# Spectral mixing, maxima scans and softmax attention in one loop of equal two-step rounds over five single PSUM banks

## The chip, the cores and the metric

The kernel runs on one core of one Trainium2 chip. The metric is the device time of one execution in microseconds (us). Five engines work at once, each through its own queue in order: TensorE (PE, matrix products; its weight loads are shown apart as PEld), VectorE (DVE), ScalarE (ACT), GpSimd (POOL) and SyncE (SP, which here only starts transfers). Matrix products are written to PSUM, which holds eight banks of 128 x 512 floats.

## The reference

One input x of 2048 rows and 512 columns goes through two mixers, and a gate per row blends them. `A_wqkv` and `A_wo` are multiplied by 64 in the set-up, so the scores are large and the softmax needs its row maxima.

```python
g = _sigmoid((x * gate_w).sum(-1, keepdims=True))
# A: softmax attention, 32 heads of width 16
q, k, v = (x @ wqkv) split in three, per head
scores = jnp.einsum("bhqd,bhkd->bhqk", q, k) * scale
p = _softmax(scores, axis=-1)
a = (p @ v over the heads) @ wo
# B: Fourier mixing, real part of a two-dimensional transform
ar = jnp.einsum("bsd,ed->bse", x, dft_hid_re)
ai = jnp.einsum("bsd,ed->bse", x, dft_hid_im)
b = jnp.einsum("ts,bse->bte", dft_seq_re, ar) - jnp.einsum("ts,bse->bte", dft_seq_im, ai)
return g * a + (1 - g) * b
```

## The kernel before

All products but one kind take operands split in two parts, hi and lo, and add three products (hi*hi, hi*lo, lo*hi). They contract over at most 64 rows, so PE is used as two row groups: j=0 in rows 0 to 63 and j=1 in rows 64 to 127. The two matmuls of a pair, one for each group, are issued side by side and run together, each with its own PSUM bank. The text counts such pairs. The exception is the product of probabilities and values (`pv`): it contracts over 128 rows, its output has 17 columns (16 values and the sum), and four of them, one for each `(c, j)`, run side by side in column groups and add up in one bank, `pvb`.

The work of a head pair p (16 of them) on PE: 64 "scans", each a pair of 128 x 512 score blocks whose row maxima are needed before the exponentials can be taken; then 32 "steps" (two query halves h, sixteen key blocks kb). A step has two score pairs (c=0 and 1), four 128 x 512 blocks of exponentials on ACT, and one `pv` group. The scans of a head pair must be done, and its maxima stored and loaded again as extra rows of the operands, before its steps begin. The spectral part has 2 phases (real and imaginary) of 16 output blocks t, each 48 pairs long (16 blocks s, three products); its coefficients are loaded in units of 4 blocks s and split into hi and lo ahead of use. At the end, the attention output is multiplied by `wo` (`mix_heads`, `mix_rest`) and added to the spectral rows.

The order of the work is written out by hand; the queues follow it. It has three parts.

1. Projections (960 pairs: q, k, v and the two hidden transforms). From the ninth block on, scans are put between the products by `beside`, one after every `PACE` = 3.9 product pairs. These scans are plain: one bank pair (`s1`), one DVE maximum over 128 x 1024 (L136).
2. 24 of the 32 spectral blocks, 1152 pairs, with 500 more scans between them, one after every 2.19 product pairs. These are "folded": ACT copies the positive part of one 128 x 512 block to SBUF (L157), and one DVE instruction folds the next block into it and takes the maximum (L159); every block has a single bank of its own (`d0`, `d1`, `k0`, `k1`). After parts 1 and 2 a total of `FRONT` = 692 of the 1024 scans are done.
3. A loop of 512 steps. Each step issues the score pair c=0 into a double bank (one ACT instruction over 1024, L220), while scans are left one scan pair, the score pair c=1 into two single banks of three (two ACT instructions of 512, L687), and the `pv` group of the step before (L693). From step `MIX` = 333, when no scans are left, the eight other spectral blocks and then the output products fill the place, three pairs a step, and `pv` is issued for two steps at once every other step.

After each query half, `quotients` (L702, L705) copies `pvb` to SBUF and sends its sums out through POOL's queue, and some steps later `divide` (L711 to L728) inverts them, brings them back through two transfers, multiplies and stores the rows. Most of `divide` is in POOL's queue. In part 3 the coefficient units are split on DVE (L809, L810).

Of the kernel before, what the change touches and what calls it, by code (L numbers as in the profile page):

```python
# [18 lines left out]
P = 128  # L19
S = 2048  # L20
# [14 lines left out]
LATER = 8  # L35
FRONT = 564 + 16 * LATER
PACE = 3.9
FOLDED = range(3 * SCANS, FRONT)
FOLD_PACE = 2.19
NARROW = 5.3  # L40
NWARM = 20
MIX = TOTAL - FRONT + 1
OUT = MIX + NB * LATER
SLOW = 3
SCANS_IN = 0
AHEAD = (9, 11, 14)


def build(tc, x, xT, wqkv, wo, wrT, wiT, cr, ci, gate, out):
    nc = tc.nc  # L50
    with ExitStack() as ctx:
        keep = ctx.enter_context(tc.tile_pool(name="keep", bufs=1))
        stk = ctx.enter_context(tc.tile_pool(name="stk", bufs=6))
# [4 lines left out]
        psf = ctx.enter_context(tc.tile_pool(name="psf", bufs=1, space=PSUM, reuse_waits="tile"))  # L58
# [3 lines left out]
        ks_d = [dram.tile([P, S], F32, name=f"ks_d{f}") for f in range(ND)]  # L62
        kf_d = [dram.tile([P, 2, S], F32, name=f"kf_d{f}") for f in range(ND)]
        m_d = [dram.tile([2, 4, 2, NB, 32], F32, name=f"m_d{p}") for p in range(NP)]
        ab_d = [[dram.tile([P, D], F32, name=f"ab_d{i}_{t}") for t in range(NB)] for i in range(2)]
        y_d = [dram.tile([P, 4, D], F32, name=f"y_d{c}") for c in range(NC)]
# [19 lines left out]
        scanned, used, unfolded = {}, {}, {}  # L86

        def row_loads(p, queue, keys=k_d):

            qs = stk.tile([P, S], F32R, tag="stk", name="qs")  # L90
            ks = stk.tile([P, S], F32R, tag="stk", name="ks")
# [9 lines left out]
        def load_scan(p):  # L101
            if p < NP:
                scanned[p], loads = row_loads(p, nc.sync)
                for load in loads:
                    load()

        def load_use(p):
            if p < NP:
                used[p], loads = row_loads(p, nc.sync)
                for load in loads:  # L110
                    load()
                qs, ks = used[p]
                for j in range(2):
                    b = 64 * j + 48
                    nc.sync.dma_start(ks[b:b + 2, :].bitcast(F32), ones_d)
                    for n in range(2):
                        nc.sync.dma_start(qs[b + n:b + n + 1, :].bitcast(F32),
                                          m_d[p][n:n + 1, :, j].rearrange("n g b k -> n b g k"))
# [6 lines left out]
        def scan(n, ps):  # L125

            p, i = n // SCANS, n % SCANS
            qb, c = i // 4, i % 4
            qs, ks = scanned[p]
            if i == 0:  # L130
                new_maxima(p)
            for j in range(2):
                b = 64 * j
                nc.tensor.matmul(ps[:, j, :], qs[b:b + 48, qb * P:(qb + 1) * P],  # L134
                                 ks[b:b + 48, c * 512:(c + 1) * 512], start=True, stop=True)
            nc.vector.tensor_reduce(mx[p][:, :, qb, c], ps, axis=AX.X, op=ALU.max)  # L136

        fold = [None, None]

        def scan_folded(n, j, bank, pool):  # L140

# [3 lines left out]
            if i == 0 and j == 0:  # L147
                new_maxima(p)
                if p == FRONT // SCANS:
                    nc.gpsimd.memset(mx[p], -3.0e38)  # L150
# [4 lines left out]
            if c % 2 == 0:  # L155
                fold[j] = pool.tile([P, 512], F32, tag=f"fold{j}", name="fold")
                nc.scalar.activation(fold[j], ps, AF.Relu)  # L157
            else:
                nc.vector.tensor_tensor_reduce(out=fold[j], in0=ps, in1=fold[j], scale=1.0, scalar=-3.0e38,  # L159
                                               op0=ALU.add, op1=ALU.max, accum_out=mx[p][:, j, qb, c // 2:c // 2 + 1])  # L160

        def shift(p):
# [10 lines left out]
            of = mx[p].rearrange("p j b c -> p (j b) c")[:, :, 0:2 if p * SCANS in FOLDED and (p + 1) * SCANS <= FRONT else 4]  # L173
# [15 lines left out]
        turns = [0]  # L189

        def wide(i, name):
            return psf.tile([P, 2, 512], F32, tag=f"wide{i}", name=name)

# [7 lines left out]
        both = []  # L201

        def qk(p, h, kb, c, pss):

            q0 = h * 1024 + c * 512
            qs, ks = used[p]
            for j in range(2):
                b = 64 * j
                nc.tensor.matmul(pss[j], ks[b:b + 50, kb * P:(kb + 1) * P],  # L209
                                 qs[b:b + 50, q0:q0 + 512], start=True, stop=True)  # L210

        def qk_both(p, h, kb, c=0):

            ps = wide(1 - SCANS_IN, "s3")
            qk(p, h, kb, c, [ps[:, j, :] for j in range(2)])
            if len(both) < 4:
                both.append(ring4.tile([P, 2, 512], F32, tag="c", name="eb"))
            e = both[ebs[0] % 4]
            ebs[0] += 1
            nc.scalar.activation(e, ps, AF.Exp, scale=SCALE)  # L220
            return [e[:, j, :] for j in range(2)]

        ebs, ahead, sums = [0], [], []

# [3 lines left out]
        with ExitStack() as pf:  # L228

            def s1():  # L230
                return pss1[0].tile([P, 2, 512], F32, tag="s1", name="s1")

            pss1 = []

            def xy():
                turns[0] += 1
                ps = wide(turns[0] % 2, "xy")
                return ps[:, 0, :], ps[:, 1, :]
# [15 lines left out]
            def load_scan_beside(p):  # L254
                scanned[p], loads = row_loads(p, nc.scalar if p else nc.sync, kf_d if p * SCANS in FOLDED else k_d)
                for n, load in enumerate(loads):
                    after(7 * n, load)
# [4 lines left out]
            def beside():  # L262
# [6 lines left out]
                if seen[0] == FOLDED[0] and not beds:  # L269
                    pace[1] = 0.0  # L270
                while seen[0] < FRONT and pace[1] >= 1.0:
                    pace[1] -= 1.0
                    n = seen[0]
                    if n % SCANS == 36 and n - n % SCANS + SCANS < FRONT:
                        load_scan_beside(n // SCANS + 1)
                    if n not in FOLDED:
                        done = scan_plain(n)
                    else:

                        scan_folded(n, 0, *beds)  # L280
# [8 lines left out]
            beds = []  # L289

            def behind(n):
                if n in FOLDED:
                    scan_folded(n, 1, *beds)
                    return n

            def scan_plain(n):
                if not beds:
                    scan(n, s1())
                    return n
                p, i = n // SCANS, n % SCANS  # L300
                qs, ks = scanned[p]
                for j in range(2):
                    ps, b = beds[0](f"{'dk'[n % 2]}{j}"), 64 * j
# [27 lines left out]
            coef = []  # L331
            for ph, plain, pair in ((0, range(NB - 2), (NB - 2, NB - 1)), (1, range(2, NB), (0, 1))):
                split_up = [(ph, t, u) for half in range(2) for t in pair for u in (2 * half, 2 * half + 1)]
                whole = [(ph, t, u) for t in plain for u in range(NU)]
                coef += split_up + whole if ph else whole + split_up
            coef = coef[:len(coef) - NU * LATER]
            craw, ready = {}, {}

            def load_coef(n, raw):
                ph, t, u = coef[n]  # L340
                craw[n] = raw
                nc.sync.dma_start(raw, (cr, ci)[ph][t, :, u * CS:(u + 1) * CS, :])

# [707 lines left out]
```

## Time and profile before

| | |
|---|---|
| runs | 1746.61, 1746.79, 1747.98 us; median 1746.79 |
| profiled execution, span | 1747.7 us |
| granted PE clock | 0.998 of full speed |
| part 1 | 0 to 289.6 us |
| part 2 | 289.6 to 688.5 us |
| part 3 with scans | 688.5 to 1328.0 us |
| part 3 with spectral blocks and outputs | 1328.0 to 1728.5 us |
| after the last round | 1728.5 to 1747.7 us |

The span of the profiled execution is 0.9 us above the median of the runs and inside their spread, so sums are made against 1747.7. PE is marked busy almost everywhere; a busy PE need not be at its peak, since a matmul's record also covers its waits inside the engine. What counts is how far the starts of pairs lie apart. An idle time in a row stands in square brackets with what ended it.

### The profile page before, as it was taken

The page shows a single profiled execution, that of the slowest core. Times are in us where ns is not written, and L with a number is a line of the kernel's source. Part 1 is how long each engine was busy: PE and PEld are TensorE (multiplying, and loading weights), DVE is VectorE, ACT ScalarE, POOL GpSimd, SP SyncE. Part 2 cuts the span into 40 slices and gives each one's busy share as a digit, 9 for nine tenths or more (in the row PEclk, how much of TensorE's full clock was granted, in tenths as well). Part 3 has the DMA queues.
Part 4 walks back from the last instruction along what each step waited for, and adds up shares of the span by engine and source line. Part 5 has one row for each costly group of instructions (what it writes and reads, how often), then busy time and mean ns, then how long its engine had stood idle before and what let it go on. Part 6 is the DMA issues. An engine that isn't in the chain of part 4 may idle for free.

```text
span 1747.7 us, 35504 instructions
## 1 busy us (share of the span) xinstructions
PE 1717.2 (98%) x13640; PEld 1020.7 (58%) x13640; DVE 1154.7 (66%) x1876; ACT 1451.8 (83%) x2383; POOL 712.4 (41%) x814
## 2 busy tenths in 40 slices
PE   8999999999999999999999999999999999999998
PEld 6887787888888887333333333333334555555554
DVE  6799999999999887666666666666664212222333
ACT  5445345888888787999999999999999888888885
POOL 3678667555556664032323323232232322322222
PEclk9999999999999999999999999999999999999999
DMA  8792666343345445432332513515313254255712
GB/s 293 258 299 77 191 196 210 114 118 116 102 151 151 140 133 112 82 65 57 60 65 56 90 34 71 87 24 96 78 35 74 65 116 90 69 141 139 175 36 100
DMA packets 126809, 199.54 MB, mean 114 GB/s; under 512 B 54016, under 2 KB 56560, under 8 KB 119728
## 3 DMA queue, kind: packets, MB, share of 16 engines
q1 hardware_dynamic: 84368, 161.02, 35.0%
q0 software_dynamic: 38496, 19.47, 5.1%
q10 hardware_dynamic: 3776, 16.78, 3.6%
q8 instruction: 107, 1.75, 0.4%
q14 instruction: 62, 0.51, 0.1%
HBM read 133.04 MB, written 63.71 MB: 113 GB/s over the span
## 4 chain that ended last, share of the span: by engine, by line
PE 86%; DMA 5%; DVE 3%; POOL 2%; issue 2%; ACT 1%; SPq 0%; DVEq 0%; POOLq 0%; ACTq 0%
PE pvb L693 27%; PE xy L184 21%; PE s L209 18%; PE s L184 8%; PE s L153 7%; PE s L134 6%; DMA lc<-ob 2%; DVE mx L136 2%; DMA fa<-ks_d 1%; DMA kf_d<-fa 1%; POOL s L252 1%; DMA raws<-xT 1%; DMA raws<-wqkv 0%; POOL el L252 0%; POOL fa L252 0%
## 5 line engine op out<-in xcount | busy, mean ns | idle before, releaser
L136 DVE TENSOR_REDUCE mx<-s 128x2 f32<-128x1024 f32 x524 | 627.1, 1222 | 204.6 <-PE s L134 204.6
L220 ACT ACTIVATE eb<-s 128x1024 f32<-128x1024 f32 x513 | 575.6, 1122 | 55.7 <-PE s L209 55.5
L687 ACT ACTIVATE e<-s 128x512 f32<-128x512 f32 x1022 | 604.4, 699 | 2.1 <-PE s L209 2.1
L693 PE MATMUL pvb<-eb,va 128*17 128x512 f32 x2052 | 515.9, 597 | 0.0
L693 PE MATMUL pvb<-e,va 128*17 128x512 f32 x2044 | 515.0, 597 | 0.0
L209 PE MATMUL s<-qs,ks 50*128 50x512 f32 x2048 | 427.2, 436 | 0.0
L209 PEld LDWEIGHTS s<-qs,ks 50*128 50x128 f32 x2048 | 210.2, 184 | 367.8 <-ACT eb L220 279.1
L184 PE MATMUL xy<-b,c 64*128 64x512 f32 x2640 | 418.4, 393 | 0.3 <-ACT c L318 0.3
L159 DVE CUSTOM_DVE_ANT_0 fold<-s,fold 128x512 f32<-128x512 f32 x500 | 338.5, 690 | 38.4 <-PE s L153 18.8
L157 ACT ACTIVATE fold<-s 128x512 f32<-128x512 f32 x500 | 295.7, 601 | 69.8 <-PE s L153 43.3
L184 PEld LDWEIGHTS xy<-b,c 64*128 64x128 f32 x2640 | 296.7, 187 | 19.9 <-ACT c L318 0.6
L153 PE MATMUL s<-ks,qs 48*128 48x512 f32 x1000 | 224.5, 405 | 6.7 <-DVE mx L159 5.1
L134 PE MATMUL s<-ks,qs 48*128 48x512 f32 x1048 | 223.1, 396 | 6.2 <-DVE mx L136 4.7
L705 POOL DMA_DIRECT2D lc<-ob x124 | 63.1, 515 | 304.7 <-DVE ob L702 304.3
L693 PEld LDWEIGHTS pvb<-eb,va 128*17 128x17 f32 x2052 | 69.1, 95 | 192.1 <-issue 183.4
L153 PEld LDWEIGHTS s<-ks,qs 48*128 48x128 f32 x1000 | 121.5, 184 | 46.4 <-DVE mx L159 17.4
L712 POOL DMA_DIRECT2D r_d<-lc x31 | 18.1, 585 | 293.3 <-DVE lc L711 284.5
L350 POOL TENSOR_TENSOR c<-craw,c 128x512 fp32r<-128x512 f32 x92 | 120.0, 1304 | 7.4
L134 PEld LDWEIGHTS s<-ks,qs 48*128 48x128 f32 x1048 | 108.0, 183 | 18.0 <-DVE mx L136 9.1
L349 POOL CAST c<-craw 128x512 fp32r<-128x512 f32 x92 | 56.3, 612 | 141.2 <-PE xy L184 137.3
L184 PE MATMUL xy<-w,b 64*128 64x512 f32 x768 | 105.2, 392 | 0.2 <-ACT s L414 0.2
L436 ACT ACTIVATE tx<-xy 128x512 f32<-128x512 f32 x48 | 28.7, 598 | 76.0 <-PE xy L184 50.2
(126 smaller groups left out, 1527.4 us busy)
## 6 DMA issues: line engine op xcount, KB each, us to landing
craw<-ci SPq DMA_DIRECT2D x64, 256.0 KB
craw<-cr SPq DMA_DIRECT2D x60, 256.0 KB
ks<-k_d SPq DMA_DIRECT2D x46, 256.0 KB
qs<-q_d SPq DMA_DIRECT2D x46, 256.0 KB
ab_d<-ab SPq DMA_DIRECT2D x32, 256.0 KB
y_d<-y SPq DMA_DIRECT2D x32, 256.0 KB
o_d<-oh POOLq DMA_DIRECT2D x28, 256.0 KB, 9.7
o_d<-ol POOLq DMA_DIRECT2D x28, 256.0 KB, 11.4
```

The source lines that it names most:

```text
L134: nc.tensor.matmul(ps[:, j, :], qs[b:b + 48, qb * P:(qb + 1) * P], ks[b:b + 48, c * 512:(c + 1) * 512], start=True, stop=True)
L136: nc.vector.tensor_reduce(mx[p][:, :, qb, c], ps, axis=AX.X, op=ALU.max)
L153: nc.tensor.matmul(ps, qs[b:b + 48, qb * P:(qb + 1) * P], ks[b:b + 48, c * 512:(c + 1) * 512], start=True, stop=True)
L157: nc.scalar.activation(fold[j], ps, AF.Relu)
L159: nc.vector.tensor_tensor_reduce(out=fold[j], in0=ps, in1=fold[j], scale=1.0, scalar=-3.0e38, op0=ALU.add, op1=ALU.max, accum_out=mx[p][:, ...
L184: nc.tensor.matmul(ps[j], lhs[r], rhs[r], start=first, stop=last)
L209: nc.tensor.matmul(pss[j], ks[b:b + 50, kb * P:(kb + 1) * P], qs[b:b + 50, q0:q0 + 512], start=True, stop=True)
L220: nc.scalar.activation(e, ps, AF.Exp, scale=SCALE)
L350: sub(lo, raw, hi.bitcast(F32))
L687: nc.scalar.activation(e[j], pss[j], AF.Exp, scale=SCALE)
L693: nc.tensor.matmul(pvb[r:r + VC, :], va[:, kb, 2 * p + j, :], es[c][j], start=kb == 0, stop=kb == NB - 1, tile_position=(0, r))
L705: nc.gpsimd.dma_start(lc[32 * n:32 * n + 32, :], ob[r + DH:r + VC, :].rearrange("p (s e) -> p s e", e=16))
```

## The change

All 32 spectral blocks move into the loop, and of the scans only 320 (`FRONT = 5 * SCANS`) stay ahead of it: 64 plain ones, now with two DVE maxima of 512, and 256 folded ones, all between the projections, the folded ones one after every 2.08 product pairs, the first scan 22 product pairs earlier than before. Part 2 is gone. The loop runs over 256 rounds of two steps. A round issues the eight score matmuls of its two steps (`e`), up to four scan pairs (`c`, plain, each matmul with a DVE maximum of 512 of its own), and 6, 7 or 9 pairs of spectral or output products (`s`), in an order given by `ORDERS` for the numbers of scan pairs and product pairs; the two matmuls of a pair are separate entries, so that one row group may be ahead of the other. Then it issues the `pv` groups of the two steps of the round before.

PSUM in the loop is eight single banks: `pvb`, `z0` and `z1` for the products of the two row groups, and `b0` to `b4` for scores and scans together. `Banks` keeps the planner's own clock and gives each score or scan the bank that it takes to be free first. Every exponential is one ACT instruction of 512 into one of 15 tiles.

The built order holds 157 rounds with three scan pairs, 57 with four, 3 with one or two and 39 with none (17 of these with six product pairs, 3 with seven, 19 with nine), in all 704 scan pairs, 1024 score pairs and 1725 product pairs.

The coefficient units are split on POOL (L214, L215). The hi and lo parts of the second phase's operands are made on POOL during the first phase (`part_b`, L872, L873), stored to `bs_d`, and loaded when the first phase's last block has used the old ones (`renew`). Row operands are loaded when two of six slots come free (`prefetch`). In the projections the sums of two key blocks are formed from tiles that are still on the chip instead of being loaded again (`fold_keys`). The scratch for POOL's transfers is set to 8192.

```diff
-FRONT = 564 + 16 * LATER
+FRONT = 5 * SCANS
 PACE = 3.9
-FOLDED = range(3 * SCANS, FRONT)
-FOLD_PACE = 2.19
+FOLDED = range(SCANS, FRONT)
+FOLD_PACE = 2.08
+MACROS = STEPS // 2
+ORDERS = {
+    (3, 7): "e1 c0 s1 e0 c1 s0 e1 s0 s1 s0 c1 s0 e0 s1 s0 c1 s0 e1 s1 c0 s1 s0 e0 s1 s1 e0 c0 e1",
+    (3, 6): "e1 c0 e1 s0 s0 e0 c1 s0 s1 s1 c0 e0 s1 s1 e0 c1 s0 s1 s0 e1 e0 e1 s0 s1 c0 c1",
+    (4, 6): "c1 e0 e0 e1 s1 c0 s0 s1 s1 e0 c1 s0 c1 s0 e1 s0 c0 e1 c0 s1 s1 s0 s0 e1 s1 c0 e0 c1",
+    (4, 7): "c0 e1 c1 s0 e0 e1 s1 s0 s0 s1 c1 e0 s1 s0 c1 s0 e0 e1 s0 c0 s1 e0 s1 s1 s0 c0 e1 s1 c1 c0",
...
+}
...
-                after(84, scan_at, PACE)
+                after(62, scan_at, PACE)
...
+            def scan_plain(n):
...
+                for j in range(2):
+                    ps, b = narrow(f"{'dk'[n % 2]}{j}"), 64 * j
+                    nc.tensor.matmul(ps, qs[b:b + 48, i // 4 * P:(i // 4 + 1) * P],
+                                     ks[b:b + 48, i % 4 * 512:(i % 4 + 1) * 512], start=True, stop=True)
+                    nc.vector.tensor_reduce(mx[p][:, j, i // 4, i % 4:i % 4 + 1], ps, axis=AX.X, op=ALU.max)
...
+            for tag in ("b0", "b1", "b2", "b3", "z0", "z1", "b4"):
+                bank(tag)
+            pvb = bank("pv", "pvb")
...
+            class Banks:
+
+                slot, late, gap, load, group = 230.0, 434.0, 106.0, 200.0, 854.0
+                period, release = {"e": 477.0, "c": 600.0}, {"e": 750.0, "c": 740.0}
...
+                    s = max(self.t, self.rows[j])
+                    if kind != "s":
+                        b = min(range(5), key=lambda b: self.free[b])
+                        s = max(s, self.free[b])
+                        a = max(self.engine[kind], s + self.late)
+                        self.engine[kind], self.free[b] = a + self.period[kind], a + self.release[kind]
+                    self.t, self.rows[j] = s + 4.0, s + self.slot
...
+            def score(j):
...
+                ps = bank(banks.take("e", j))
+                nc.tensor.matmul(ps, ks[b:b + 50, kb * P:(kb + 1) * P], qs[b:b + 50, q0:q0 + 512],
+                                 start=True, stop=True)
...
+            def scan(j):
...
+                ps = bank(banks.take("c", j))
+                nc.tensor.matmul(ps, qs[b:b + 48, qb * P:(qb + 1) * P], ks[b:b + 48, c * 512:(c + 1) * 512],
+                                 start=True, stop=True)
+                nc.vector.tensor_reduce(mx[p][:, j, qb, c:c + 1], ps, axis=AX.X, op=ALU.max)
...
+                        def leave(s=s, w=w, i=i):
+                            if w == 0 and i == 0 and (ph, t, s) != (0, 0, 0):
+                                split_unit()
+                                load_unit(ap, "craw", 2)
+                            if i == 2 and t == NB - 1:
+                                freed.append((ph, s))
...
+            for m in range(MACROS):
+                for step in (2 * m, 2 * m + 1):
+                    if halved and halved[0][0] <= step:
+                        p_, h_ = halved[0][1][:2]
+                        divide(*halved.pop(0)[1])
...
+                    part_b(step)
...
+                count_ = max(0, min(4, want - n, ready - n))
+                for k, token in enumerate(order(count_, sizes[m])):
+                    {"e": score, "c": scan, "s": fill}[token[0]](int(token[1]))
+                    if late and k in (6, 13, 20):
+                        late.pop(0)()
+                for step in ((2 * m - 2, 2 * m - 1) if m else ()):
+                    pv(step)
```

More of the change, by code (lines that the diff above doesn't have):

```diff
@@ L123, in new_maxima, with scan_folded @@
             mx[p] = sm.tile([P, 2, NB, 4], F32, tag="mx", name="mx")
[L125 to L136, printed above, removed]
         fold = [None, None]
-        def scan_folded(n, j, bank, pool):
+        def scan_folded(n, j, bank):
             p, i = n // SCANS, n % SCANS
@@ L895, in build @@
+            assert min(scans) == TOTAL, scans
+            for step in (STEPS - 2, STEPS - 1):
+                pv(step)
             groups = {}
```

750 lines of the change are left out of this document (352 added, 398 removed), and 4 rows, old and new, of the table ORDERS.

## The prediction

> **What bounds the kernel now.** I read the stages first (busy time of each engine in each stretch: length, then PE, PEld, DVE, ACT, POOL with instruction counts), then the costly groups, then single rounds in order of time.
>
> ```profile
> core 0: us, PE busy (x) PEld busy (x) DVE busy (x) ACT busy (x) POOL busy (x), PEclk, DMA share, GB/s
> 0.00:58.30 58.30, 51.36 (x411) 39.82 (x411) 30.07 (x52) 32.62 (x64) 19.82 (x21) 1.00 0.87 296
> 58.30:289.60 231.30, 226.52 (x1922) 187.04 (x1921) 227.71 (x208) 105.86 (x211) 168.91 (x133) 1.00 0.65 203
> 289.60:688.50 398.90, 392.17 (x3265) 337.53 (x3262) 358.79 (x1041) 326.34 (x569) 228.60 (x226) 1.00 0.46 131
> 688.50:1328.00 639.50, 635.69 (x4693) 238.22 (x4693) 428.68 (x401) 633.20 (x1000) 189.14 (x282) 1.00 0.33 62
> 1328.00:1728.50 400.50, 400.50 (x3286) 212.40 (x3286) 99.31 (x162) 349.11 (x536) 101.23 (x150) 1.00 0.42 102
> 1728.50:1747.70 19.20, 10.98 (x78) 5.73 (x74) 10.12 (x14) 4.65 (x8) 4.70 (x4) 0.94 0.39 144
> ```
>
> PE looks full in every stage, so it does not tell them apart; the second-busiest engine does. Beside plain scans it is DVE (227.7 of 231.3), beside folded ones DVE and ACT (359 and 326 of 399), in the loop with scans ACT (633 of 640). Only from 1328 on is PE alone. The clock is full.
>
> Two-step rounds already exist there. The timeline of PE, one round:
>
> ```profile
> 1402.28 0.73 PE L209 MATMUL s<-qs,ks 50*128 50x512 f32 x4
> 1402.85 0.63 PE L184 MATMUL s<-b,chi 64*128 64x512 f32 x4
> ...
> 1404.23 0.66 PE L209 MATMUL s<-qs,ks 50*128 50x512 f32 x4
> 1404.81 0.61 PE L693 MATMUL pvb<-eb,va 128*17 128x512 f32 x2
> ...
> 1406.65 0.73 PE L209 MATMUL s<-qs,ks 50*128 50x512 f32 x4
> ```
>
> Ten pairs and two `pv` groups take 1406.65 - 1402.28 = 4.37 us. From 1402.85 to 1404.23 six pairs go by: 0.23 each. The first two pairs take 0.57, so the first costs 0.11 more; the last two take 0.58 until `pv` starts, 0.12 more; from `pv` to the next round are 1.84. Hence a round whose last pair starts L after its first takes 1.84 + 0.11 + 0.35 + L = 2.30 + L, with L = 0.23 x (pairs - 1) while nothing is waited for (2.07 for ten).
>
> **What the change moves.** It is one exchange: 1152 spectral pairs leave part 2 for the loop, 372 more scans too, and part 2's 399 us go. In return the loop's 333 one-step rounds (639.5/333 = 1.92 us each) and its two-step rounds (400.5 us) become 256 fuller ones. Fewer switches between pairs and `pv` are the gain: 256 for some 423 now. The new cost is waiting for banks.
>
> *Turn of a bank.* All scores and scans share five banks, so the sixth use must wait until the first is read. The next rows give each leg: scan pair and its DVE start; a fold's end, the weight load that waited for it, its matmul; then groups with mean ns.
>
> ```profile
> 901.10 0.40 PE L134 MATMUL s<-ks,qs 48*128 48x512 f32 x2
> 901.54 1.23 DVE L136 TENSOR_REDUCE mx<-s 128x2 f32<-128x1024 f32 x1 [0.66 <-PE s L134]
> 902.23 1.10 ACT L687 ACTIVATE e<-s 128x512 f32<-128x512 f32 x2
> ```
> ```profile
> 300.87 0.08 DVE L159 DVE_READ_ACCUMULATOR2_ANT mx<- 128x1 f32 x1
> 301.01 0.18 PEld L153 LDWEIGHTS s<-ks,qs 48*128 48x128 f32 x2 [0.16 <-DVE mx L159]
> 301.11 0.41 PE L153 MATMUL s<-ks,qs 48*128 48x512 f32 x2
> ```
> ```profile
> L136 DVE TENSOR_REDUCE mx<-s 128x2 f32<-128x1024 f32 x524 | 627.1, 1222 | 204.6 <-PE s L134 204.6
> L687 ACT ACTIVATE e<-s 128x512 f32<-128x512 f32 x1022 | 604.4, 699 | 2.1 <-PE s L209 2.1
> L159 DVE CUSTOM_DVE_ANT_0 fold<-s,fold 128x512 f32<-128x512 f32 x500 | 338.5, 690 | 38.4 <-PE s L153 18.8 <-ACT fold L157 8.2 <-POOL mx L150 1.3
> L157 ACT ACTIVATE fold<-s 128x512 f32<-128x512 f32 x500 | 295.7, 601 | 69.8 <-PE s L153 43.3 <-DVE mx L159 4.7 <-DVE mt L175 0.3
> L436 ACT ACTIVATE tx<-xy 128x512 f32<-128x512 f32 x48 | 28.7, 598 | 76.0 <-PE xy L184 50.2 <-POOL ab L533 15.8 <-PE s L134 5.1
> L702 DVE COPY ob<-pvb 128x512 f32<-128x512 f32 x31 | 21.4, 692 | 71.3 <-PE pvb L693 69.6
> L830 DVE SCALAR_TENSOR_TENSOR y<-s,gm,y 128x512 f32<-128x512 f32 x16 | 12.0, 751 | 61.1 <-PE s L184 60.8
> ```
>
> Matmul to reader 901.54 - 901.10 = 0.44. A DVE maximum over 512 has no row; L702 and L159, which read one bank too, take 0.69 (half of L136, 0.61, is the floor, since fixed parts don't halve). From a reader's end (300.95) to the weight load 0.06, from load to matmul 0.10. A scan's turn is 0.44 + 0.69 + 0.16 = 1.29, a score's (0.60 to 0.70 on ACT) 1.20 to 1.30. So use n can't start before use n-5 plus about 1.29. The planner's own table lets a matmul start the moment the bank is free (434 + 740 = 1.17 us); the load that can't be made ahead of its wait, 0.10, is not in it.
>
> *Walk through a (3, 6) round*, in order: uses 1 to 5 (e c e e c) start at 0, 0, 0.23, 0.69, 0.69. Use 6 waits for the first banks: 1.29. Use 7 follows in the same row group at 1.52, use 8 at 1.75, use 9 (c, behind two s) at 1.98, 10 at 2.44, 11 at 2.58 (6 + 1.29), 14 at 1.98 + 1.29 = 3.27. L is 3.27 where 13 pairs alone give 2.76: the round takes 5.57, not 5.06. For (3, 7) the last use falls at about 3.2 likewise, beside 2.99. With four scan pairs there are 16 uses, and the sixteenth is three turns behind the first: L = 3 x 1.29 = 3.87, period 6.17, beside 5.29 (six products) and 5.52 (seven). I take 5.55 and 6.15.
>
> ACT and DVE themselves are not the bound: eight exponentials at 0.50 (two in 1.10, one 0.60) make 4.0, eight maxima at 0.69 make 5.5, below 5.55 and 6.15. The Trainium skill (TensorEngine Tiling, "PSUM Bottleneck") says that tiling speeds up TensorE and not the emptying of PSUM, which may become the bottleneck. The trace agrees as far as the first loop stage goes (ACT 633 of 640 us). Read as a rate alone, the rule would add nothing to the sum here (1324 us); read as a wait for each bank, it gives the 1422 below.
>
> *Loop sum.* 157 x 5.55 = 871; 57 x 6.15 = 351; without scans 17 x 4.4, 3 x 4.6 and 19 x 5.05 = 185; 3 x 5.0 = 15: 1422 us. Without any bank wait it would be 256 x 2.07 + 3453 pairs x 0.23 = 1324.
>
> *POOL.* Coefficient splits go to its queue, behind `divide`; the page's and timeline's rows:
>
> ```profile
> 739.60 0.57 POOL L712 DMA_DIRECT2D r_d<-lc  x1 [10.45 <-DVE lc L711]
> ...
> 749.46 0.82 POOL L728 DMA_DIRECT2D o_d<-ol  x1
> ```
> ```profile
> L350 POOL TENSOR_TENSOR c<-craw,c 128x512 fp32r<-128x512 f32 x92 | 120.0, 1304 | 7.4
> L349 POOL CAST c<-craw 128x512 fp32r<-128x512 f32 x92 | 56.3, 612 | 141.2 <-PE xy L184 137.3 <-PE s L153 2.7 <-DMA craw<-cr 1.1
> o_d<-ol POOLq DMA_DIRECT2D x28, 256.0 KB, 11.4
> ```
>
> A `divide` holds POOL 749.46 + 0.82 - 739.60 = 10.7 us; a split is 1.92. A unit of 12 pairs lasts 12/7 x 5.55 = 9.5 us. A split queued behind a `divide` is ready 12.6 us after it began, so up to 3.1 us late, if its unit began in those 3.1 us: one time in three, 0.5 us on average, 31 times: 16. `part_b` reuses the tiles that `o_d` transfers read, and these land after 11.4 us; splits behind it slip as well. I take 25 in all, bounds 0 and 100. That also bounds the smaller scratch for POOL's transfers, which no row shows.
>
> *Front.* 960 + 320 pairs would be 294 us. Scans start 22 product pairs sooner: 58.3 - 5 = 53. The 64 plain scans have two maxima of 512 for one of 1024: DVE 1.22 to 1.38 each, and PE comes by only every 4.9 x 0.23 = 1.13: 83. The 256 folded ones now share ACT with the projections. Per scan ACT has 0.59 (295.7/500) and, each 12 products or 5.77 scans, two copies of 0.60 and about one cast: 1.75/5.77 = 0.30; sum 0.89, against 0.71 of PE (3.08 x 0.23). By starts 0.50 apart it is 0.74. Bounds 256 x 0.74 = 189 and 256 x 0.90 = 231. Part 2, with only 0.65 of ACT and 0.72 of DVE per scan, already ran at 0.80 (398.9/500) where PE needs 0.73. I take 0.84: 215. Changing over the banks (all eight are allotted anew; before, scores were issued ahead): 4. Front: 355, bounds 325 and 375.
>
> *Priced at nothing.* The second operands' 16 loads, 32 stores and 32 loads of 256 KB on SP's queue: transfers fill 0.33 to 0.42 of the loop now, and each has several rounds until its use. `quotients` and the spectral rows' scaling on DVE (0.69, 0.75) lie under `pv`, as blocks end with a round; uncovered they would cost one round in seven 0.7, about 25. After the loop the same work: 20.
>
> *Sum:* 355 + 1422 + 25 + 20 = 1822 for 1747.7; against the median, 0.9 less, still about 1820.
>
> **Rivals.**
> 1. *Banks are free in time* (faster). If a turn is shorter or falls under the products of the orders, rounds take 2.30 + 0.23 per pair: loop 1324 to 1346, front 335, tail 20, so 1680 to 1700. For it: products stand between the uses. Against: four-scan rounds need three turns whatever the order. It decides below 1747.7 - 355 - 25 - 20 - 1324 = 24 us of bank waits, 0.11 per round with scans; the walk gives (1422 - 1324)/214 = 0.46.
> 2. *POOL becomes the bound in the loop's first half*: splits late at every `divide` (near the 100) and folded scans at 0.90: 1860 to 1900. Against: POOL is busy about half of the loop by these rows.
> 3. *Row groups issued apart don't run apart.* Orders hold 5 (three scans), 9 or 11 (four) neighbours in the same row group; if each lost the 0.11 of a load, 1470 x 0.11 = 160: 1980. Against: a row group's matmuls follow at 0.23 now, so its next load already runs under its own matmul. The Trainium skill (TensorE: Matmul & The Clock Gate, "Part 3", what overlaps) has loads overlap matmuls only in another row group, which would be this rival; its Part 2 also allows loads to the background buffer, and the 0.23 agrees with that. By the first the time would be the 1980, by the second the sum stands.
> 4. *The change only shifts time* (bank waits near half of mine): 1750 to 1785.
>
> **How the numbers follow.** My case (1785 to 1850) 0.52, rival 2 0.14, rival 3 0.02, rival 4 0.12, rival 1 with lesser forms 0.18, within 0.2% 0.02. A change under 0.2% can't be told from none here. Slower 0.80, same 0.02, faster 0.18. The range 1695 to 1875 leaves out rival 3, the end of rival 2 and the best of rival 1; my case alone is 1785 to 1850.
>
> **What would show it.** Right: first score near 355 us; ACT over 0.85 busy from 136 us until then; rounds with four scan pairs 6.1 apart, with three 5.5; some 100 us of idle weight loads at L592 and L621 ended by DVE and ACT, fewer by POOL. Wrong: three-scan rounds at 5.3 or less, a front of 330, or idle before the products (L829) ended by POOL or transfers.

## The result and the profile after

The changed kernel takes 1935.45 us (median of 4 runs, 1932.77 to 1937.69) against 1747.38 us before (4 runs, 1746.61 to 1748.34). The ratio is 1.1069, with a 95% interval from 1.1054 to 1.1085: 188 us slower. The forecast of 1820 had the sign, but the time lies outside its range of 1695 to 1875. The profiled execution has a span of 1934.6 us.

The stages of the changed kernel, as the busy time of each engine in each stretch (columns as in the prediction; the last two numbers are the share of the DMA engines and GB/s):

```profile
0.00:136.00 136.00, 127.09 (x995) 99.57 (x995) 108.79 (x179) 67.53 (x129) 84.44 (x72) 0.97 0.72 245
136.00:363.20 227.20, 205.38 (x1585) 158.17 (x1587) 177.48 (x533) 204.41 (x399) 99.77 (x79) 1.00 0.39 109
363.20:1917.60 1554.40, 1469.94 (x11005) 776.15 (x11001) 1026.89 (x1644) 1095.14 (x2053) 563.84 (x724) 0.96 0.39 93
1917.60:1934.60 17.00, 9.09 (x66) 5.37 (x58) 10.14 (x14) 2.55 (x5) 4.84 (x4) 0.91 0.42 156
```

The stretches are the plain scans with their products, the folded scans, the loop, and the end. The front takes 363.2 us (forecast 355), the end 17.0 (20). The loop takes 1554.4, where the forecast had 1422 + 25 = 1447: 107 of the 113 us by which the profiled span exceeds the forecast sum of 1822 lie there. The granted clock in the loop is 0.96, where before it was full.

Most rounds run as forecast. One view of PE's timeline shows the first matmul of four rounds in a row, and then a stall:

```profile
673.75 0.49 PE L592 MATMUL s<-qs,ks 50*128 50x512 f32 x1
...
679.32 0.49 PE L621 MATMUL s<-ks,qs 48*128 48x512 f32 x1
...
685.43 0.49 PE L592 MATMUL s<-qs,ks 50*128 50x512 f32 x1
...
691.00 0.49 PE L592 MATMUL s<-qs,ks 50*128 50x512 f32 x1
...
692.31 0.49 PE L621 MATMUL s<-ks,qs 48*128 48x512 f32 x1
698.89 0.79 PE L829 MATMUL z<-b,chi 64*128 64x512 f32 x1 [6.09 <-POOL chi L214]
699.48 0.63 PE L592 MATMUL s<-qs,ks 50*128 50x512 f32 x1
...
706.78 0.49 PE L592 MATMUL s<-qs,ks 50*128 50x512 f32 x1
```

The starts are 5.57 (three scan pairs), 6.11 (four) and 5.57 us apart; the round after them takes 706.78 - 691.00 = 15.78. Over all rounds, from the starts of their first matmuls, the medians are 5.58 (65 rounds of three scan pairs and six products), 5.57 (90, three and seven), 6.11 (57, four), 4.43 and 5.06 (without scans, six and nine products). Counts times medians make 1425 us; the forecast had 1422. Most of what is missing is in a few rounds: 19 of them are more than 0.8 us over the median of their kind, by 117 us together.

What PE waited for in that round stands in the timeline of POOL's queue:

```profile
678.63 0.58 POOL L640 DMA_DIRECT2D r_d<-lc  x1 [5.54 <-DVE lc L639]
689.77 1.93 POOL L642 DMA_DIRECT2D rb<-r_d  x4 [10.57 <-DMA r_d<-lc]
693.32 1.26 POOL L643 TENSOR_TENSOR ob<-ob,rb 128x512 f32<-128x512 f32 x1 [1.61 <-DMA rb<-r_d]
...
697.40 0.82 POOL L656 DMA_DIRECT2D o_d<-ol  x1
698.21 0.62 POOL L214 CAST chi<-craw 128x512 fp32r<-128x512 f32 x1
```

`divide` sends the inverted sums out at 678.63 and may read them back only when they have landed; POOL stands still for 10.57 us, the division ends at 697.40 + 0.82, and only then comes the coefficient split (L214) on which PE's next product waits. This `divide` held POOL for 19.6 us. Before, the same step waited 1.70:

```profile
741.87 1.95 POOL L714 DMA_DIRECT2D rb<-r_d  x4 [1.70 <-DMA r_d<-lc]
...
749.46 0.82 POOL L728 DMA_DIRECT2D o_d<-ol  x1
```

Measured in this way, 28 `divide`s before held POOL for 10.4 to 14.7 us; of 28 after, nine held it for 16.6 to 19.8. What went on during that wait is in the view of the DMA engines from 678 to 690 (transfers with KB each and us from issue to landing):

```profile
q1 hardware_dynamic: 583, 1.58, 82.8%
...
ks<-k_d SPq DMA_DIRECT2D x1, 128.0 KB, 11.6
...
r_d<-lc POOLq DMA_DIRECT2D x1, 8.0 KB, 10.9
```

Queue q1, which carries SP's transfers, filled 82.8% of the sixteen engines, mostly with the row operands that `prefetch` loads, and the 8 KB of the sums landed 10.9 us after their issue. The list of waits of the changed kernel (total us, times, longest) has both ends of it, and the banks:

```profile
PEld s L621 <- DVE mx L623: 113.1, 392, 3.0
POOL rb L642 <- DMA r_d<-lc: 104.1, 31, 10.6
POOL ob L643 <- DMA rb<-r_d: 73.8, 30, 5.4
PEld z L829 <- POOL chi L214: 64.8, 12, 12.5
PE z L829 <- POOL chi L214: 60.1, 12, 12.2
PEld s L592 <- ACT eb L580: 47.8, 77, 0.9
PEld s L592 <- ACT e L580: 39.9, 64, 0.9
PE s L621 <- DMA qs<-q_d: 13.5, 2, 7.4
```

The fourth and fifth row are the same twelve stalls, seen by the weight loads and by the matmuls; they must not be added. (The 137 us in two expectations below is such a sum, 64.8 + 60.1 with 12.6 for the lo parts of the splits.) Eight of them are longer than 2.5 us. Six of these eight follow a `divide` that held POOL for over 16 us, one (at 593 us) a `divide` of 13.0 us behind a split that a `part_b` wait of 10.0 us had made late, and one (at 458 us) a `part_b` wait of 10.0 us for its operand that began 2 us after a `divide` of 10.4. The last row is a second kind of stall: twice the first scan of a new head pair waited for its own row operand. In the group list after, the maxima over 512 are shown to take 686 ns; 0.69 was put together from other groups:

```profile
L623 DVE TENSOR_REDUCE mx<-s 128x1 f32<-128x512 f32 x1408 | 907.4, 686 | 354.2 <-PE s L621 199.6
```

So the theory for the experiments was that rounds and front are as forecast, and that the excess is POOL's queue, held by the return trip of the sums through the DMA queues, with a double buffer of split coefficients too small to bridge it. Where an expectation below speaks of A, it is this theory; B is the case that the loss lies elsewhere, as the expectation itself spells out. The rivals were that POOL is only a symptom and the same time is lost to other waits when the splits come in time, that the orders are at fault, and that row groups issued apart do not run apart.

### The profile page after: what moved, and what is told of

Read it like the earlier page. It is cut to its first block, busy times and chain, and to the rows that moved or that the text cites. A ratio compares the mean times of both kernels' runs of the same rounds, so it can differ in the third digit from the quotient of the medians.

```text
span 1934.6 us, 36943 instructions
## 1 busy us (share of the span) xinstructions
PE 1811.5 (94%) x13640; PEld 1039.3 (54%) x13640; DVE 1323.3 (68%) x2367; ACT 1369.6 (71%) x2583; POOL 752.9 (39%) x878
## 3 DMA queue, kind: packets, MB, share of 16 engines
q8 instruction: 107, 1.75, 0.4%
## 4 chain that ended last, share of the span: by engine, by line
PE 67%; DMA 9%; POOL 8%; DVE 5%; ACT 4%; issue 4%; DVEq 0%; POOLq 0%; ACTq 0%; SPq 0%
PE pvb L602 20%; PE z L829 16%; PE s L592 14%; PE s L621 11%; DMA r_d<-lc 4%; PE xy L188 3%; PE s L157 3%; DVE mx L623 2%; DMA rb<-r_d 2%; ACT fold L161 2%; POOL el L244 1%; DMA o_d<-ol 1%; POOL s L244 1%; POOL rb L642 1%; POOL clo L215 1%
## 5 line engine op out<-in xcount | busy, mean ns | idle before, releaser
L623 DVE TENSOR_REDUCE mx<-s 128x1 f32<-128x512 f32 x1408 | 907.4, 686 | 354.2 <-PE s L621 199.6
L580 ACT ACTIVATE eb<-s 128x512 f32<-128x512 f32 x1094 | 609.5, 602 | 267.9 <-PE s L592 106.5
L592 PE MATMUL s<-qs,ks 50*128 50x512 f32 x2048 | 697.6, 430 | 0.6 <-DVE mx L623 0.3
L829 PE MATMUL z<-b,chi 64*128 64x512 f32 x2060 | 589.4, 407 | 60.1 <-POOL chi L214 60.1
L621 PE MATMUL s<-ks,qs 48*128 48x512 f32 x1408 | 586.5, 454 | 18.8 <-DMA qs<-q_d 13.5
L829 PEld LDWEIGHTS z<-b,chi 64*128 64x128 f32 x2060 | 333.8, 190 | 85.7 <-POOL chi L214 64.8
L829 PE MATMUL z<-b,clo 64*128 64x512 f32 x1030 | 370.8, 410 | 2.4 <-POOL clo L215 1.5
L621 PEld LDWEIGHTS s<-ks,qs 48*128 48x128 f32 x1408 | 248.0, 187 | 198.7 <-DVE mx L623 113.1
L163 DVE CUSTOM_DVE_ANT_0 fold<-s,fold 128x512 f32<-128x512 f32 x256 | 172.3, 690 | 49.2 <-ACT fold L161 38.8
L829 PEld LDWEIGHTS z<-b,clo 64*128 64x128 f32 x1030 | 185.6, 189 | 21.3 <-POOL clo L215 11.1
L215 POOL TENSOR_TENSOR clo<-craw,chi 128x512 fp32r<-128x512 f32 x126 | 161.5, 1281 | 32.5 <-PE z L829 15.6
L214 POOL CAST chi<-craw 128x512 fp32r<-128x512 f32 x126 | 77.4, 614 | 238.6 <-PE z L829 150.7
L157 PE MATMUL s<-ks,qs 48*128 48x512 f32 x512 | 135.3, 421 | 21.8 <-ACT fold L161 20.3
```

Source lines behind the costliest of these rows:

```text
L157: nc.tensor.matmul(ps, qs[b:b + 48, qb * P:(qb + 1) * P], ks[b:b + 48, c * 512:(c + 1) * 512], start=True, stop=True)
L214: copy(hi, raw)
L215: sub(lo, raw, hi.bitcast(F32))
L592: nc.tensor.matmul(ps, ks[b:b + 50, kb * P:(kb + 1) * P], qs[b:b + 50, q0:q0 + 512], start=True, stop=True)
L621: nc.tensor.matmul(ps, qs[b:b + 48, qb * P:(qb + 1) * P], ks[b:b + 48, c * 512:(c + 1) * 512], start=True, stop=True)
L623: nc.vector.tensor_reduce(mx[p][:, j, qb, c:c + 1], ps, axis=AX.X, op=ALU.max)
```

## The experiments

**A third buffer for the split coefficients.** One change: every third split goes to a buffer of its own, and splits are issued one unit of 12 pairs earlier.

```diff
-                hi, lo = (cw.tile([P, 512], F32R, tag=tag, name=tag).rearrange(...)
-                          for tag in ("chi", "clo"))
+                made[0] += 1
+                pool, tags = (more[0], ("chi3", "clo3")) if made[0] % 3 == 0 else (cw, ("chi", "clo"))
+                hi, lo = (pool.tile([P, 512], F32R, tag=tag, name=tag).rearrange(...)
+                          for tag in tags)
...
-                            if w == 0 and i == 0 and (ph, t, s) != (0, 0, 0):
+                            if w == 0 and i == 0:
```

> Edit: a third pair of coefficient tiles, and every unit split one unit earlier; nothing else. Theory A (splits stand in POOL's queue behind the inversions, which wait for small transfers; 19 rounds lose 117 us so): the slack grows by one unit of 9.5 us, most of the 137 us of idle weight loads that POOL ends at the products goes, and the time falls by 80 to 115 us to 1820 to 1855. Theory B (the coefficient transfers themselves are late): the splits still wait for their data, the raw tiles are as many as before, and the time falls by less than 40 us. Rounds with three and four scan pairs keep their medians of 5.57 and 6.11 us under both.

Measured: 1856.27 us (1851.57 to 1859.24), ratio 1.0610 [1.0588, 1.0631]: 79 us less than the change as made, just short of the 80 expected. Three rows of its list of waits:

```profile
PEld s L625 <- DVE mx L627: 116.2, 408, 3.0
POOL rb L646 <- DMA r_d<-lc: 104.2, 31, 10.8
PEld z L833 <- POOL chi L217: 2.5, 2, 2.0
```

The transfers are as late as before (104.2 us), the banks cost as much, and the wait of products for a split has fallen from 64.8 to 2.5 us. The rounds keep their medians (5.57, 5.58, 6.11); ten of them are over by 39.5 us together. So the late split is a cause and no symptom. What is left is two waits of about 10 us for the row operands of scans (`PE s` ended by `qs<-q_d`, 19.6 us for both) and their after-effects.

**The splits on DVE.** They leave POOL's queue, and stand between the maxima instead.

```diff
-        def split_unit(copy=nc.gpsimd.tensor_copy, sub=nc.gpsimd.tensor_sub):
+        def split_unit(copy=nc.vector.tensor_copy, sub=nc.vector.tensor_sub):
```

> Edit: the coefficient splits go to DVE in the loop, as in the kernel before. Theory A: products no longer wait for POOL (137 us to under 15), but 126 splits of 0.4 and 0.7 us stand in DVE's queue among the maxima, each holding banks up to 1.1 us longer: plus 60 to 110 us of waits of scores and scans for DVE. Together 1900 to 1960 us. Theory B: the late transfers now stop DVE and with it all banks: over 1980 us.

Measured: 1924.08 us (1921.71 to 1926.45), ratio 1.1007 [1.0982, 1.1031]. From its list of waits:

```profile
PEld s L592 <- DVE mx L623: 115.2, 146, 2.3
```

In the kernel as changed this wait was 20.8 us. No long stall on a split is left, but a pair of splits delays the maxima, and with them the release of banks: 79 rounds are over their median, by 102 us together. The loss only changes its place. DVE has time in the mean (76% busy in this run), but not within a bank's turn.

**The loads later.** The row operands of the next head pair are loaded from the ninth round of a head pair's sixteen on, not from the fifth, so that they meet fewer `divide`s.

```diff
-                    elif want_use and i >= 8:
+                    elif want_use and i >= 16:
```

> Edit: the row operands of the next head pair are loaded from the 16th step of a head pair on instead of the 8th, so that their 14 transfers are not issued in the same round as an inversion. Theory A: the small transfers of every second inversion come back sooner, POOL's waits for them (104 and 74 us in all, longest 10.6) fall by a third or more, rounds that lost 8 to 15 us there lose little, and the time falls by 20 to 60 us. Rival (small transfers are slow by themselves, or the scan loads are to blame): no change within 10 us.

Measured: 1915.09 us (1910.28 to 1920.72), ratio 1.0956 [1.0931, 1.0982]: 20 us less. Its list of waits:

```profile
POOL rb L642 <- DMA r_d<-lc: 59.7, 31, 6.2
PEld z L829 <- POOL chi L214: 40.9, 9, 12.7
```

The wait for the sums falls from 104.1 to 59.7 us, and no wait is longer than 6.2. That the loads delay the sums is shown by this. But it gives only 20 us, the least that was expected: three `divide`s still hold POOL over 15 us (15.3 to 18.5), and two stalls, at 459 and 724 us, follow waits of 9.8 and 11.5 us of `part_b` for the block that it makes into the second operand. POOL's queue has more than one step that waits for a transfer.

**No return trip.** The sums are neither sent out nor brought back, so the attention rows are not divided by them; the rest of `divide` stays.

```diff
-                nc.gpsimd.dma_start(r_d[p][h].rearrange("n (s e) -> (n s) e", e=16), lc)
-                for n, (c, j, r) in enumerate(quads):
-                    nc.gpsimd.dma_start(rb[r:r + DH, :], r_d[p][h][n:n + 1, :].to_broadcast([DH, 512]))
```

> Edit: the inverted sums are neither sent out nor brought back (five small transfers and POOL's waits for them go), so the attention rows are not divided by their sums; the rest of the inversion stays in POOL's queue, and so do the splits and their transfers. Theory A (the return trip of the small transfers is what holds the splits up): an inversion holds POOL 5 us instead of 11 to 21, the rounds that lost more than 0.8 us fall from 19 with 117 us to under 8 with 30, the granted clock rises above 0.985, and the time falls by 80 to 115 us to 1820 to 1855. Theory B (coefficient transfers, or the multiply and copy work on POOL itself): it falls by under 40 us.

Measured: 1831.66 us (1828.90 to 1834.42), ratio 1.0479 [1.0427, 1.0530]: 104 us less. Its front, loop and end:

```profile
0.00:365.20 365.20, 334.10 (x2581) 259.32 (x2583) 286.21 (x711) 272.21 (x527) 184.31 (x150) 0.99 0.52 159
365.20:1814.70 1449.50, 1437.23 (x11001) 764.55 (x11001) 1025.93 (x1644) 1094.02 (x2053) 486.35 (x569) 0.99 0.40 97
1814.70:1831.80 17.10, 9.12 (x66) 5.36 (x58) 10.13 (x14) 2.55 (x5) 4.86 (x4) 0.91 0.42 155
```

The loop takes 1449.5 us, 104.9 less than with the trip. Four rounds are over, by 11.6 us. The waits of `part_b` are still there, and cost nothing now:

```profile
POOL oh L869 <- DMA braw<-ab_d: 48.3, 8, 10.8
```

In this run single waits of POOL of up to 10.8 us are bridged; each of the eight long stalls of the changed kernel followed a wait within a `divide` or next to one. That is no strict rule: with the later loads, the stall at 724 us followed a wait of 11.5 us of `part_b`, and the last `divide` had ended 36 us before. The two waits of scans for row operands are gone too, so the 104.9 hold everything that follows from the trip, not POOL's part alone; the third buffer puts that part at 79.

**A quarter of each maximum.** Each DVE maximum of the loop reads 128 of its 512 columns. This leaves out three quarters of the maxima.

```diff
-                nc.vector.tensor_reduce(mx[p][:, j, qb, c:c + 1], ps, axis=AX.X, op=ALU.max)
+                nc.vector.tensor_reduce(mx[p][:, j, qb, c:c + 1], ps[:, 0:128], axis=AX.X, op=ALU.max)
```

> Edit: each maximum in the loop is taken over 128 of its 512 columns; three quarters of the maxima are left out, matmuls and their order stay. Bank theory (use n waits for use n-5 plus a turn of 1.29 us): a scan's turn falls to about 0.9 us while a score's stays at 1.2 to 1.3, so rounds with four scan pairs fall from 6.11 to about 5.8 and those with three from 5.57 to about 5.45; waits of scans and scores for DVE (113 and 21 us) vanish. Rival (the orders themselves or the separate issue set the rounds): medians stay within 0.05 us. The POOL term stays, so the time falls by 20 to 50 us.

Measured: 1897.96 us (one run). The group of maxima and two waits:

```profile
L623 DVE TENSOR_REDUCE mx<-s 128x1 f32<-128x128 f32 x1408 | 397.8, 291 | 795.5 <-PE s L621 511.6
```
```profile
PEld s L592 <- ACT eb L580: 66.7, 176, 0.9
PEld s L621 <- ACT eb L580: 36.6, 126, 0.9
```

With 291 ns for 686 the rounds fall from 5.58 to 5.42 and 5.57 to 5.48 (three scan pairs) and from 6.11 to 5.95 and 5.96 (four), less than the 5.8 expected. So the read of a bank is on the path, as the walk had it. But of 0.40 us less per turn only 0.1 to 0.16 arrives per round: the waits for DVE are gone from the top of the list and waits for ACT, the scores' readers, grow in their place. By the prediction's sum a score's turn is nearly as long as a scan's (1.20 to 1.30 for 1.29 us), so a shorter scan turn leaves the scores' turns as the bound. This reading agrees with the two rows; no run shortens the scores' turns to test it.

**Four banks for five.**

```diff
-                        b = min(range(5), key=lambda b: self.free[b])
+                        b = min(range(4), key=lambda b: self.free[b])
```

> Edit: the planner may use four of the five shared banks. Bank theory: use n waits for use n-4 plus a turn of 1.29 us, so the 16th use is three turns and more behind the first one's row and the 13th exactly three: rounds with three scan pairs go from 5.57 to 6.2 to 6.6, those with four from 6.11 to 6.7 to 7.1, those without scans to 4.5 to 4.9; the time rises by 130 to 240 us. Rival (the separate issue of the row groups, or the engines behind the banks, set the rounds): under 0.2 us for each round, under 50 us in all.

Measured: 2133.43 us (one run), 198 more. Rounds take 6.71 and 6.62 (three scan pairs), 7.35 and 7.37 (four), and even rounds without scans take 4.92 for 4.43, all up to 0.3 us above the expected ranges. The medians alone add 258 us; in return 11 rounds lose 54 us in place of 19 that lost 117. Two groups of weight loads, with what ended their idle time:

```profile
L592 PEld LDWEIGHTS s<-qs,ks 50*128 50x128 f32 x2048 | 344.6, 186 | 389.5 <-DVE mx L623 193.5
L621 PEld LDWEIGHTS s<-ks,qs 48*128 48x128 f32 x1408 | 256.9, 188 | 215.5 <-DVE mx L623 106.7
```

The number of banks sets the rounds: the fifth is worth 1.05 to 1.26 us of a round with three or four scan pairs. This is the step on which the forecast of the loop rested.

**Row groups side by side.** The orders keep only their entries of row group 0, and each is issued for both groups.

```diff
-                for k, token in enumerate(order(count_, sizes[m])):
+                tokens = [t[0] + j for t in order(count_, sizes[m]) if t[1] == "0" for j in "01"]
+                for k, token in enumerate(tokens):
```

> Edit: the two matmuls of each pair are issued side by side again, in the order in which the first row group had them. Rival of the prediction (row groups issued apart lose the load, 0.11 us at each of 1470 neighbours of one row group): the time falls by 100 us or more. Bank theory: a pair takes two banks at once, so five banks hold two pairs and the third waits a full turn; rounds grow by 0.4 to 0.9 us and the time rises by 100 to 200 us.

Measured: 2095.20 us (one run), 160 more; rounds of 6.37, 6.25, 7.43 and 6.92, and 4.89 without scans. From its list of waits:

```profile
PEld s L621 <- ACT eb L580: 118.7, 239, 1.7
```

In the kernel as changed this wait was 17.8. So issue apart is no loss here, and the prediction's third rival falls. The sign is that of the bank theory (a pair takes two banks at once), though rounds of four scan pairs with six products grew by 1.32 us where 0.9 was the most expected. That the other row group goes on while one waits is not shown: in the changed kernel no weight load of either group starts between 674.56 and 675.06 us, and then one of each starts at once.

**A front of four head pairs.** 64 scans move from the front into the loop.

```diff
-FRONT = 5 * SCANS
+FRONT = 4 * SCANS
...
-FOLD_PACE = 2.08
+FOLD_PACE = 2.77
```

> Edit: 256 scans ahead of the loop and not 320 (64 plain, 192 folded, one after every 2.77 product pairs), the other 64 in the loop. Theory (ACT bounds the front, 0.84 us for a folded scan, where PE alone needs 0.71): the first score falls from 363 to 310 to 330 us, the loop gains 64 scan pairs at 0.4 to 0.55 us, 25 to 35 us; the time falls by 0 to 25 us. Rival (the front is bound by PE, 0.23 us for each of its pairs): the first score falls by 15 us only, and the time rises by 10 to 25 us.

Measured: 1934.50 us (1926.14 to 1938.70), ratio 1.1055 [1.1025, 1.1085], the same as the change as made. The folded stretch:

```profile
136.00:327.10 191.10, 180.49 (x1459) 147.89 (x1457) 135.50 (x402) 168.37 (x336) 100.18 (x79) 0.99 0.41 121
```

It ends 36 us sooner for 64 scans fewer, though each of the 192 folded ones left takes 191.1/192 = 1.00 us for 0.89. The loop has 112 rounds of four scan pairs for 57, so that its medians sum to 1459 us for 1425. What the front saves (36 us), the loop pays (34).

**All together.** Third buffer, later loads, new orders for the rounds with three and four scan pairs, and a planner that adds the 0.10 us of the load behind each wait.

```diff
-                        s = max(s, self.free[b])
+                        s = max(s, self.free[b] + 104.0)
...
-                    elif want_use and i >= 8:
+                    elif want_use and i >= 16:
...
-    (3, 6): "e1 c0 e1 s0 s0 e0 c1 s0 s1 s1 c0 e0 s1 s1 e0 c1 s0 s1 s0 e1 e0 e1 s0 s1 c0 c1",
+    (3, 6): "e1 c0 c1 s0 e0 s1 s0 s1 s1 e0 c0 e1 s0 s1 c0 e1 s0 s0 s1 e0 s1 c1 s0 e1 c1 e0",
...
```

> Edit: the third coefficient buffer, the later row loads, and orders for three and four scan pairs that were chosen with the weight load's 0.10 us after a bank comes free, which the planner now adds too. Bank theory: five turns bound the rounds whatever the order, so three-scan rounds fall from 5.57 to 5.4 to 5.5 and four-scan rounds from 6.11 to 6.0 to 6.1, 15 to 30 us; with 79 and some 10 to 20 us of the other two edits 1800 to 1840 us, still slower than the kernel before. Rival (the orders were at fault): three-scan rounds at 5.3 or less, four-scan rounds at 5.6, under 1790 us.

Measured: 1841.67 us (1838.90 to 1844.21), ratio 1.0539 [1.0522, 1.0556]. It is the best version that computes everything, and still 94 us above the kernel before; the expected range ended at 1840. The new orders and planner together bring rounds of three scan pairs from 5.57 to 5.47; those of four stay at 6.11. Against these orders the ones as built cost 0.1 us a round, some 16 us in 155 rounds. That no order does better follows from the bank theory and was not tested beyond these two sets.

## Why the prediction was wrong in size

*Rounds and bank turns: right.* "I take 5.55 and 6.15": 5.57 and 6.11. "4.4, 4.6, 5.05" without scans: 4.43, 4.66, 5.06. The loop sum without stalls was given as 1422, and 1425 follows from the medians. The 1.29 us of a turn rested on 0.69 for a maximum, and 0.686 was measured; four banks and the quarter maxima show that turns set the rounds. Rival 1 (banks free in time) is out with that: 1425 less 1324 is 101 us of bank waits. The indicator given for it (some 100 us of idle weight loads) was poor: three rows alone make 113.1 + 47.8 + 39.9 = 201 us, since a load may wait while PE still works off what was loaded (the load at 675.06 us had waited 0.31 us, and a matmul ran until 675.18). Only the distance of rounds measures it.

*Front: right within its bounds.* 363.2 for 355. The folded scans began where 53 + 83 = 136 had them (the tile's row: count, ns, first and last start):

```profile
L161 ACT ACTIVATE fold<-s x256: 577/600/634, 137.3 to 361.8; 128x512 f32<-128x512 f32 x128
```

They took 227.2/256 = 0.89 us each for the 0.84 taken. ACT was busy for 204.4 of the 227.2 us, 0.90, above the 0.85 named. The term that was mis-sized is the choice of 0.84 between two sums of ACT's work: the larger, 0.59 + 1.75/5.77 = 0.89, was the right one. With the front of four head pairs 12 products stand beside 12/2.77 = 4.33 folded scans; the same sum gives 0.59 + 1.75/4.33 = 0.99, and 1.00 was measured, although ACT had less to do in all. The agreement is luck in part: ACT was busy for 204.4/256 = 0.80 us per scan, and for 168.4/192 = 0.88 with the front of four, so the sum gives the time but puts ACT's work too high. What fills the rest of a folded scan's time stays open.

*POOL: the step that failed.* It read: "A split queued behind a `divide` is ready 12.6 us after it began, so up to 3.1 us late ... one time in three ... I take 25 in all, bounds 0 and 100." The frequency was near: 12 stalls for 31 inversions, though two of the eight long ones began with a wait of `part_b`, which the sum named and did not price by itself. The size was not. The 10.7 us of a `divide` came from one row of the kernel before, and were taken over; nine of 28 now take 16.6 to 19.8, so a split came up to 12.5 us late, and 64.8/12 = 5.4 on average. Taking the trip away gives 104.9 us back in the loop: that is the term with all that hangs on it, just beyond its upper bound. One of the prediction's own signs of being wrong, idle before the products (L829) ended by POOL, is what came.

*"Priced at nothing": wrong in the same way.* The loads for `ks` and `qs` were given several rounds until their use, and their share of the DMA engines was read as a mean (0.33 to 0.42; the loop has 0.39). They come in bursts, one of which filled 82.8% of the engines for twelve microseconds, and a mean hides that the 8 KB on which POOL stands still are issued into such a burst. In the code both are released by the position in the head pair: `divide` comes nine steps after the half, `prefetch` begins with the fifth round. The loads were late for PE itself too, twice, for 13.5 us.

*Slow clock: not in the sum at all.* The 19 long rounds lose 117 us, while the waits named above make about 64.8 + 13.5 = 78. The remaining 40 us or so, an estimate by that difference, agree with what the last section shows of the clock; no run separates the clock from what else a stall leaves behind.

*Rival 2* (POOL becomes the bound in the loop's first half, 1860 to 1900) was nearest: the right queue, but it is no bound by rate (POOL is busy for 39% of the span), and the stalls do not end with the first half: the last long ones fall at 1576 and 1686 us. Rivals 3 and 4 did not happen.

*Tail:* 17.0 for 20.

With the trip gone the kernel takes 1831.7 us, 0.6% above the forecast. That it comes so near is luck in part: the forecast holds 25 us for POOL, and this loop has 1449.5 - 1425 = 24.5 us of other losses in their place. What remains above the kernel before is the loss which the exchange itself brings. The loop without the long stalls (1449.5) is 409.5 longer than the old one (1728.5 - 688.5 = 1040.0), so it gives back all of part 2's 398.9 us and 11 more, and the front, with 128 scans more than part 1 had, is 75.6 longer than part 1. In part 2 a pair cost 398.9/1652 = 0.24 us (1152 product and 500 scan pairs), close to the 0.23 between pairs that wait for nothing. The 1524 pairs that moved into the loop made it 409.5 us longer, 0.27 each. They came from a stage that had hardly a gap to close.

## What to carry to other kernels

A queue that holds a wait for a transfer must be priced at that transfer's time in the new traffic, not in the old: look for what the change issues in the same microseconds, burst by burst, and give what stands behind such a wait one more buffer than its mean asks for. With shared single banks, the round follows from turns (matmul to reader, read, release, load) counted over the number of banks, and that walk was good to about 1% for the kernel as changed; with four banks the rounds lay up to 0.3 us above its ranges, and with the quarter maxima rounds of four scan pairs 0.15 us above its 5.8. Before work is moved into a loop "to fill it", compare what a pair costs where it stands with what it will cost there.

## What the runs showed of the hardware that was not expected

A stall of PE costs more than its length. The granted clock (the column behind the counts) around the stall shown above:

```profile
670.00:690.00 20.00, 20.00 (x157) 10.69 (x158) 17.08 (x28) 15.31 (x29) 2.70 (x4) 1.00 0.70 136
690.00:698.30 8.30, 2.80 (x23) 1.20 (x15) 1.97 (x3) 2.17 (x4) 6.55 (x10) 0.85 0.07 18
698.30:706.00 7.70, 6.99 (x29) 3.49 (x33) 2.07 (x3) 2.45 (x5) 1.79 (x2) 0.50 0.44 121
706.00:712.00 6.00, 6.00 (x52) 3.06 (x44) 3.85 (x6) 4.64 (x9) 3.34 (x4) 1.00 0.06 22
```

After 6.09 us without a matmul the clock is 0.50 until 706.0 us, 7.1 us after the restart at 698.89. In the 7.7 us of that row 29 matmuls go by; at full clock it was 157 in 20 us. Finer stretches show when the clock fell:

```profile
692.80:695.70 2.90, 0.00 (x1) 0.00 (x0) 0.73 (x2) 0.36 (x1) 2.24 (x3) 1.00 0.00 0
695.70:698.90 3.20, 0.01 (x1) 0.01 (x1) 0.00 (x0) 0.00 (x0) 3.14 (x4) 0.51 0.11 9
```

The last matmul had ended at 692.31 + 0.49 = 692.80, and the clock was full for 2.9 us more. The first matmul after the stall took 0.79 us; those at the starts of the rounds shown above took 0.49. The stall at 593 us is the same, in PE's timeline and in the stretch after it:

```profile
593.07 0.79 PE L829 MATMUL z<-b,chi 64*128 64x512 f32 x1 [6.83 <-POOL chi L214]
```
```profile
592.00:600.00 8.00, 6.80 (x30) 2.18 (x30) 1.38 (x2) 2.28 (x4) 4.12 (x5) 0.50 0.51 127
```

So a stall of about 6.5 us costs the round 10 (15.78 for 5.57). The Trainium skill (TensorE: Matmul & The Clock Gate, "Part 1: The HAM clock gate") has the clock go to half after at least one idle window of about 3.4 us, and back after about 3.4 us of sustained work. The first agrees with these rows to within half a microsecond (2.9 us); the way back took about twice as long at these two stalls (7.1 us at the first).

A small transfer took nearly as long as the burst it was issued into: 8 KB took 10.9 us from issue to landing in a burst of 82.8%, where in the kernel before 2.3 us (741.87 - 739.60) passed from the same issue to the step that waits for its landing.
